# A transformer block in 32-token segments: three of four row tiles turned by DMA, the last MLP quarter finished tile by tile

## Chip, cores and metric

One core of one Trainium2 chip runs the kernel. The metric is device time in microseconds (us), a median over runs. A trace is one profiled execution. Engines: PE is TensorE (PEld its weight loads), DVE VectorE, ACT ScalarE, POOL GpSimd, SP SyncE, which only issues DMAs. A q behind the name (SPq, ACTq, POOLq) is the engine's queue of waits and DMA issues. "L497" is line 497 of the kernel before.

## What is computed

A recurrent attention over 64 segments of 32 tokens and an MLP read the same normalized rows, and both are added to the input. All is in bfloat16.

```python
x = A_x                                     # 1 x 2048 x 1024
xn = _layernorm(x, axis=-1)
return x + _A_ref(xn, ...) + _B_ref(xn, ...)

# _A_ref: 64 segments in order, 8 memory rows carried, 32 heads of 128
h = concatenate([mem, xs])                  # 40 x 1024
q, k, v = h @ Wq, h @ Wk, h @ Wv            # 1024 x 4096 each
p = softmax(mask(q @ k.T * scale))
o = (p @ v) @ Wo                            # 4096 x 1024
mem = o[:, :8]; outs.append(o[:, 8:])
# _B_ref
gelu(xn @ w1 + b1) @ w2 + b2                # 1024 x 3584 x 1024
```

## The kernel before

**The MLP comes first**, in four quarters of 512 rows, each of four row tiles of 128. `first_product` (L497) multiplies the 28 column blocks of w1 with the turned rows of the quarter, `xnT`, in eight matmuls each; ScalarE and VectorE make the GELU of each block. Then, in quarters 0 to 2, the second product (L618) runs tile by tile: 28 matmuls for each half of the columns, after which VectorE adds the bias (L625) and x (L626) into the x tile, and `keep_R` (L447) stores it to R_n in DRAM. In the same loop the next quarter's rows are made ready: `ln_apply` (L403) normalizes tile t, and after the tile's second half `turn_x` turns it by eight transposes on TensorE (L412) into PSUM and two copies to SBUF (L417), one on ScalarE and one on VectorE. At the quarter's end `keep_xT` stores the turned rows to DRAM (L430, L440) for the recurrence, with copies on GpSimd (L435) between, and `turn_R` (L484) issues some 14 small DMAs for each tile, which lay the sums of R_n out as the recurrence's residual rows; for the third quarter GpSimd issues them, for the fourth they go into a list `small` (L486).

The order of the work is that of the program text on each engine; DMAs leave in the order of their issuing queue. SP's queue holds at first the x rows, w1 and w2, then `keep_xT` of quarter 0, the x rows of quarter 1 (L344), 11 copies of streamed weights from DRAM to DRAM and five early weights (L246, L248), four `keep_R`, `keep_xT` and `turn_R` of the next quarter, then the next x rows, and so on.

**The last quarter** starts the recurrence's loads: each w1 block that is done with is overwritten by a weight unit of 512 KB. Its second product holds eight banks of PSUM (six named ps, two pT) for all four tiles at once. It begins with a bias matmul (ones x b2, L644) and a residual matmul (identity x x, L645) for each bank, then 28 steps of eight matmuls (L651); after each second step a w2 unit is done and `fetch_resident` loads a weight unit over it, after each fourth a gT unit. At the end eight copies (L665) on VectorE and ScalarE empty the banks, and four `keep_R` on ScalarE's queue store the rows. One of the ps banks holds the memory rows just before, until VectorE has copied them (L324).

**The recurrence** takes 64 segments. 47 of 64 weight units stay in SBUF, 17 are streamed in every segment through six places; a place is loaded again when its unit is done (`start_stream`, L278), on SP's queue. A segment makes K, Q and V in two halves (L769), scores, exponentials, and the O product (L1027); `put_mem` (L314) puts its new memory rows into the next segment's rows and marks the segment's end. Its own rows and residuals come by small loads: the next rows (L286), this segment's residuals (L1124) and, in each fourth segment, the residuals of the rows left over (L1150). VectorE adds the residuals to the output (L1184), and stores follow (L1190, L1218). The queue of these loads and stores is `loads`:

```python
loads = nc.scalar if s < EARLY_SEGS else nc.gpsimd      # EARLY_SEGS = 5
```

The list `small` is worked off by GpSimd, one or two DMAs after each streamed unit. After the last segment 12 stores, six on SP's queue and six on ScalarE's, write the output (L1207).

Of the kernel before, what the change touches and what calls it, by code (L numbers as in the profile page):

```python
# [17 lines left out]
P = 128  # L18
# [6 lines left out]
SEG = 32  # L25
# [23 lines left out]
SCRATCH = 320  # L49
SMALL = 3776  # L50
LEAD = 6
EARLY_SEGS = 5
LEAD_FIRST = 4
SCORES_0 = (6, 6, 6, 5)
SUMS_0 = (4, 4, 4, 4)
# [59 lines left out]
def kernel(  # L115
# [215 lines left out]
    with tc.tile_pool(name="ma", bufs=2) as ma, tc.tile_pool(name="mps", bufs=6, space=PSUM) as mps:  # L331
# [39 lines left out]
        for i in range(14):  # L371
            t = slab(f"w2_{i}")[:, :].rearrange("p (c d) -> p c d", d=DM)
            nc.sync.dma_start(out=t, in_=w2_v[:, 2 * i:2 * i + 2, :])
            w2_sb.append(t)

        mv = ma.tile([P, NT, 2], F32, name="ln_mv", bufs=1)
        rstd = ma.tile([P, NT], F32, name="ln_rstd", bufs=1)
# [44 lines left out]
        def turn_x(tt, xn, xnT):  # L422
            pT = turned(xn)
            for half in range(2):
                turned_out(tt, pT, half, xnT, nc.scalar.copy if (tt + half) % 2 else nc.vector.tensor_copy)

        def keep_xT(tg, xnT):
            xl = [t[:, 0:512].rearrange("p (g k i t) -> p g k i t", g=2, k=KT, i=GRP) for t in ko_flat]
            for half in range(2):
                nc.sync.dma_start(  # L430
                    out=rows_d[16 * tg:16 * tg + 16, :, 128 * half:128 * half + 128].rearrange("s p c -> p s c"),
                    in_=xnT[half].rearrange("p s k t -> p s (k t)"),
                )
                for g in range(4):
                    nc.gpsimd.tensor_copy(  # L435
                        out=xl[g // 2][:, g % 2, 4 * half:4 * half + 4, :, :],
                        in_=xnT[half][:, 4 * g:4 * g + 4, :, NX:SEG].rearrange("p i k t -> p k i t"),
                    )
            for k in range(2):
                nc.sync.dma_start(  # L440
                    out=rowsL_d[4 * tg + 2 * k:4 * tg + 2 * k + 2, :, :].rearrange("g p c -> p g c"),
                    in_=xl[k][:, :, :, :, :].rearrange("p g k i t -> p g (k i t)"),
                )

        def keep_R(ttg, rsb):
            eng = nc.scalar if ttg >= NT - 4 else nc.sync
            eng.dma_start(out=R_n[ttg * P:ttg * P + P, :], in_=rsb[:, :])  # L447

        def main_row(slot):
# [94 lines left out]
        for tg in range(4):  # L544
# [53 lines left out]
            if not last:  # L598
                xnT = new_xnT(tg + 1)
                for t in range(4):  # L600
                    xtoks[4 * tg + 4 + t] = load_x(4 * tg + 4 + t)
                if tg == 0:
                    for unit, c in copies.items():
                        fetch(c, unit)
                    fetch_resident(*EARLY)
                for t in range(4):
                    ln_stats(4 * tg + 4 + t)
                ln_sqrt(4 * tg + 4, 4 * tg + 8)
                ln_rstd(4 * tg + 4, 4 * tg + 8)
                for t in range(4):  # L610
                    ttg = 4 * tg + t
                    xn = ln_apply(ttg + 4)
                    rsb = xtoks[ttg]
                    for nb in range(2):
                        cs = slice(nb * 512, (nb + 1) * 512)
                        ps = mps.tile([P, 512], F32, name="ps")
                        for fc in range(FC):
                            nc.tensor.matmul(  # L618
                                ps[:, :],
                                lhsT=gts[fc // 4][:, fc % 4, t * P:(t + 1) * P],  # L620
                                rhs=w2_sb[fc // 2][:, fc % 2, cs],
                                start=(fc == 0),
                                stop=(fc == FC - 1),
                            )
                        nc.vector.tensor_tensor(out=ps[:, :], in0=ps[:, :], in1=b2bc[:, cs], op=ALU.add)  # L625
                        nc.vector.tensor_tensor(out=rsb[:, cs], in0=ps[:, :], in1=rsb[:, cs], op=ALU.add)  # L626
                        if nb == 1:
                            turn_x(ttg + 4, xn, xnT)
                    keep_R(ttg, rsb)
                keep_xT(tg + 1, xnT)  # L630
                for t in range(4):
                    turn_R(4 * tg + t, nc.gpsimd if tg == 2 else nc.sync)
            else:


                start_stream("xn2")
                start_stream("xn3")
                put_mem(o_sb, nxt["hT"], mps.tile([P, 512], F32, name="ps"), wide=False)
                nc.sync.dma_start(out=d_oL[:, 0:DM], in_=Wo_v[:, h + 1, :])
                pss = [mps.tile([P, 512], F32, name="ps") for _ in range(6)]  # L640
                pss += [mps.tile([P, 512], F32, name="pT", bufs=2) for _ in range(2)]
                for n in range(8):
                    cs = slice((n % 2) * 512, (n % 2 + 1) * 512)
                    nc.tensor.matmul(pss[n][:, :], lhsT=ones[0:1, :], rhs=b2row[0:1, cs], start=True, stop=False)  # L644
                    nc.tensor.matmul(  # L645
                        pss[n][:, :], lhsT=ident, rhs=xtoks[4 * tg + n // 2][:, cs], start=False, stop=False
                    )
                for fc in range(FC):
                    for t in range(4):
                        for nb in range(2):  # L650
                            nc.tensor.matmul(  # L651
                                pss[2 * t + nb][:, :],
                                lhsT=gts[fc // 4][:, fc % 4, t * P:(t + 1) * P],
                                rhs=w2_sb[fc // 2][:, fc % 2, nb * 512:nb * 512 + 512],
                                start=False,
                                stop=(fc == FC - 1),
                            )
                    if fc % 2:
                        fetch_resident(f"w2_{fc // 2}")
                    if fc % 4 == 3:  # L660
                        fetch_resident(f"gT{fc // 4}")
                for n in range(8):
                    cs = slice((n % 2) * 512, (n % 2 + 1) * 512)
                    cp = nc.scalar.copy if n % 2 else nc.vector.tensor_copy
                    cp(out=xtoks[4 * tg + n // 2][:, cs], in_=pss[n][:, :])  # L665
                for t in range(4):
                    keep_R(4 * tg + t, xtoks[4 * tg + t])

# [3 lines left out]
    with tc.tile_pool(name="late", bufs=1) as late, \  # L674
# [67 lines left out]
        for s in range(NSEG):  # L742
# [435 lines left out]
            for w, r in reversed(list(enumerate(tiles))):  # L1178
                if left_o:
                    o = psX[:, 256 * w:256 * w + 256].rearrange("p (h e) -> p h e", e=32)  # L1180
                else:
                    o = o_sb[:, 0:8, :]
                r_rows = r.rearrange("p (h e) -> p h e", e=32)
                nc.vector.tensor_tensor(out=r_rows, in0=o, in1=r_rows, op=ALU.add)  # L1184
                if left_o and not final:

                    for b in range(2):
                        c0 = 256 * (2 * b + w)
                        eng = nc.scalar if w else nc.gpsimd
                        eng.dma_start(out=outL_d[og, :, c0:c0 + 256], in_=r[64 * b:64 * b + 64, :])  # L1190
# [5 lines left out]
            if final:  # L1196
                engines = [nc.sync, nc.scalar]
                n = 0
                for w, r in enumerate(tiles):
                    for b in range(2):  # L1200
                        cs = slice(256 * (2 * b + w), 256 * (2 * b + w) + 256)
                        pieces = [(rows, slice(64 * b + m0, 64 * b + m0 + NX))]
                        for sl, row in left_rows:
                            p0 = 64 * b + NL * sl
                            pieces.append((slice(row, row + NL), slice(p0, p0 + NL)))
                        for o, i in pieces:
                            engines[n % 2].dma_start(out=out_flat[o, cs], in_=r[i, :])  # L1207
                            n += 1
            elif left_o:
                pairs = [(out_flat[rows, :], outL_d[og, m0:m0 + NX, :])]  # L1210
                pairs += [
                    (out_flat[row:row + NL, :], outL_d[og, NL * sl:NL * sl + NL, :]) for sl, row in left_rows
                ]
                for o, r in pairs:
                    small.append(lambda o=o, r=r: nc.gpsimd.dma_start(out=o, in_=r))
            else:
                for j in range(4):
                    loads.dma_start(out=out_flat[rows, 256 * j:256 * j + 256], in_=res[32 * j:32 * j + NX, :])  # L1218
# [37 lines left out]
```

## Time and profile before

| what | us |
|---|---|
| three runs | 1810.53, 1817.72, 1818.7 (median 1817.72) |
| the profiled execution | 1811.68, span 1809.9, mean granted clock 0.998 |
| MLP, span's start to the first matmul of the recurrence | 417.0 |
| TensorE busy | 1707.1 (94%) |
| VectorE, ScalarE, GpSimd busy | 978.1, 687.9, 305.2 |

The page's first part gives each engine's busy time, the second the span in 40 slices of 45 us: a digit is the busy share in tenths, PEclk the granted clock, DMA the share of the 16 DMA engines. The third part gives the DMA queues: 567.08 of 592.07 MB go through q1, SP's. The chain of work that ended last is followed back from the end; in order of time it reads as "start, length, what". A table by stretch gives the busy time of each engine between two times. In a timeline, brackets give the idle time ahead of an instruction and what ended it.

### The profile page before, as it was taken

The page shows a single profiled execution, that of the slowest core. Times are in us where ns is not written, and L with a number is a line of the kernel's source. Part 1 is how long each engine was busy: PE and PEld are TensorE (multiplying, and loading weights), DVE is VectorE, ACT ScalarE, POOL GpSimd, SP SyncE. Part 2 cuts the span into 40 slices and gives each one's busy share as a digit, 9 for nine tenths or more (in the row PEclk, how much of TensorE's full clock was granted, in tenths as well). Part 3 has the DMA queues.
Part 4 walks back from the last instruction along what each step waited for, and adds up shares of the span by engine and source line. Part 5 has one row for each costly group of instructions (what it writes and reads, how often), then busy time and mean ns, then how long its engine had stood idle before and what let it go on. Part 6 is the DMA issues. An engine that isn't in the chain of part 4 may idle for free.

```text
span 1809.9 us, 71522 instructions
## 1 busy us (share of the span) xinstructions
PE 1707.1 (94%) x31173; PEld 893.0 (49%) x31173; DVE 978.1 (54%) x2508; ACT 687.9 (38%) x1700; POOL 305.2 (17%) x595
## 2 busy tenths in 40 slices
PE   8999999998988999999999999999999999999997
PEld 4444444444444545545444555554545454555544
DVE  7657483804554555555555555555555555555554
ACT  6334260702333334333333334343433333434333
POOL 0000000411122211111111212111111111111111
PEclk9999999999999999999999999999999999999999
DMA  9931111769999999999999999999999999999997
GB/s 290 308 100 48 52 48 36 246 225 345 385 371 346 389 377 384 387 377 393 380 373 374 383 395 394 368 398 379 393 385 376 382 370 369 398 393 384 391 396 294
DMA packets 220870, 592.07 MB, mean 327 GB/s; under 512 B 46283, under 2 KB 75995, under 8 KB 220556
## 3 DMA queue, kind: packets, MB, share of 16 engines
q1 hardware_dynamic: 197652, 567.08, 83.5%
q0 software_dynamic: 17184, 17.23, 2.9%
q8 instruction: 244, 4.00, 0.9%
q10 hardware_dynamic: 5720, 3.19, 0.6%
q14 instruction: 70, 0.57, 0.1%
HBM read 573.43 MB, written 28.90 MB: 333 GB/s over the span
## 4 chain that ended last, share of the span: by engine, by line
PE 72%; DMA 13%; issue 6%; ACT 4%; DVE 3%; POOL 1%; ACTq 0%; DVEq 0%; POOLq 0%; SPq 0%
PE acc L769 34%; PE acc L1027 12%; PE ps L497 11%; PE ps L618 8%; DMA u<-Wc_O 7%; DMA u<-Wc_V 3%; PE ps L651 2%; ACT mixed L938 2%; PE acc L978 1%; DMA u<-Wc_Q 1%; PE mixed L886 1%; DVE kq L853 1%; DVE pd_main L951 1%; POOL res_d L486 1%; ACT kq L848 1%
## 5 line engine op out<-in xcount | busy, mean ns | idle before, releaser
L769 PE MATMUL acc<-u,hr_home 128*32 128x512 bf16 x11520 | 760.8, 380 | 15.7 <-issue 6.0
L769 PEld LDWEIGHTS <-hr_home 128*32 128x32 bf16 x12288 | 348.0, 96 | 285.5 <-issue 33.8
L769 PE MATMUL acc<-u,hrL 128*32 128x512 bf16 x2880 | 254.5, 380 | 4.4 <-issue 2.4
L497 PE MATMUL ps<-u 128*128 128x512 bf16 (+1 forms) x920 | 194.4, 373 | 2.0 <-ACT u L417 2.0
L267 DVE TENSOR_SCALAR u<-kept 128x512 uint32<-128x512 uint32 x254 | 163.1, 684 | 51.7 <-PE acc L769 39.2
L821 ACT CAST d_oL<-acc 128x512 bf16<-128x512 f32 x143 | 82.0, 585 | 261.0 <-PE acc L769 254.2
L618 PE MATMUL ps<-u 128*128 128x512 bf16 x672 | 147.0, 379 | 0.0
L1027 PEld LDWEIGHTS <-kq 128*32 128x32 bf16 x3908 | 103.1, 96 | 79.0 <-issue 22.2
L1027 PE MATMUL acc<-u,d_oL 128*32 128x512 bf16 x1944 | 133.9, 381 | 8.5 <-DMA u<-Wc_O 4.7
L497 PEld LDWEIGHTS <-u 128*128 128x128 bf16 x920 | 89.8, 98 | 104.9 <-issue 2.4
L1027 PE MATMUL acc<-u,kq 128*32 128x256 bf16 (+1 forms) x2372 | 117.2, 313 | 16.0 <-DMA u<-Wc_O 13.4
L853 DVE STREAM_TRANSPOSE kq<-kq 128x512 bf16<-128x512 bf16 x128 | 91.0, 711 | 74.8 <-ACT kq L848 72.6
L951 DVE TENSOR_TENSOR pd_main<-kq,mixed 128x320 bf16<-128x320 bf16 x128 | 62.4, 487 | 127.3 <-ACT mixed L938 127.3
L848 ACT CAST kq<-acc 128x512 bf16<-128x512 f32 (+2 forms) x192 | 85.3, 444 | 114.7 <-PE acc L769 85.1
L1218 POOL DMA_DIRECT2D out_dram<-hr_home x172 | 87.2, 514 | 227.3 <-DVE hr_home L1184 226.8
L825 ACT CAST kq<-acc 128x512 bf16<-128x512 f32 x128 | 75.2, 587 | 111.2 <-PE mixed L892 109.9
L769 PEld LDWEIGHTS <-hrL 128*32 128x32 bf16 x3072 | 86.3, 96 | 58.1 <-issue 5.9
L916 DVE TENSOR_TENSOR kq<-kq,mixed 128x96 bf16<-128x96 bf16 (+1 forms) x256 | 38.1, 190 | 125.7 <-ACT kq L906 70.5
L618 PEld LDWEIGHTS <-u 128*128 128x128 bf16 x672 | 65.3, 98 | 77.4 <-DVE g_u L579 0.4
L571 ACT ACTIVATE g_xb<-ps,b1col 128x512 bf16<-128x512 f32 x112 | 76.8, 686 | 55.6 <-PE ps L497 54.7
L938 ACT ACTIVATE mixed<-mixed,small_consts 128x160 f32<-128x160 f32 x256 | 94.2, 368 | 8.4
L1027 PEld LDWEIGHTS <-d_oL 128*32 128x32 bf16 x2592 | 63.8, 96 | 63.8 <-issue 16.1
(132 smaller groups left out, 2015.4 us busy)
## 6 DMA issues: line engine op xcount, KB each, us to landing
u<-Wc_K SPq DMA_DIRECT2D x256, 512.0 KB
u<-Wc_V SPq DMA_DIRECT2D x256, 512.0 KB
u<-Wc_O SPq DMA_DIRECT2D x256, 512.0 KB
u<-Wc_Q SPq DMA_DIRECT2D x192, 512.0 KB
u<-in_B_w_dram SPq DMA_DIRECT2D x28, 512.0 KB
u<-in_A_Wq_dram SPq DMA_DIRECT2D x13, 512.0 KB
u<-in_A_Wv_dram SPq DMA_DIRECT2D x12, 512.0 KB
u<-in_A_Wk_dram SPq DMA_DIRECT2D x9, 512.0 KB
```

The lines of the kernel that those rows point to most:

```text
L267: nc.vector.tensor_single_scalar(out=out, in_=in_, scalar=0, op=ALU.bitwise_or)
L497: nc.tensor.matmul(ps[:, SEG * s0:SEG * s1].rearrange("p (s t) -> p s t", t=SEG), lhsT=w1_sb[fb // 2][:, kt, (fb % 2) * P:(fb % 2 + 1) * P ...
L571: nc.scalar.activation(out=xb[:, :], in_=ps[:, :], func=ACT.Identity, bias=b1col[:, fb:fb + 1], scale=1.0)
L618: nc.tensor.matmul(ps[:, :], lhsT=gts[fc // 4][:, fc % 4, t * P:(t + 1) * P], rhs=w2_sb[fc // 2][:, fc % 2, cs], start=(fc == 0), stop=(fc ...
L769: nc.tensor.matmul(o, lhsT=lhs[:, i, :], rhs=m, start=(i == seq[0]), stop=(i == seq[-1]), tile_position=(0, 32 * j),)
L821: cp(out=out, in_=ps.rearrange("p (h e) -> p h e", e=32))
L848: nc.scalar.copy(out=q_home[:, h0:h1, NL:40], in_=ps[:, 32 * h0:32 * h1].rearrange("p (h e) -> p h e", e=32))
L853: nc.vector.transpose(out=home, in_=home)
L938: nc.scalar.activation(out=mixed[:, 160 * b:160 * b + 160], in_=mixed[:, 0:160], func=ACT.Exp, scale=-1.0, bias=off[:, b:b + 1],)
L951: nc.vector.tensor_tensor(out=pdA.rearrange("p c b q -> p b c q"), in0=prA[:, None, :, :].to_broadcast([P, 2, 4, 40]), in1=dd, op=ALU.mult,)
L1027: nc.tensor.matmul(acc[r0:r0 + rows, 0:256 * len(blocks)], lhsT=lhsT, skip_group_check=True, rhs=o_columns(t, k, blocks), start=start, sto ...
L1218: loads.dma_start(out=out_flat[rows, 256 * j:256 * j + 256], in_=res[32 * j:32 * j + NX, :])
```

## The change

- `send_x`: tiles 1 to 3 of the next quarter are turned by eight transposing DMAs each, on SP's queue, from 32 rows x 512 columns of the normalized tile straight into `xnT`. Tile 0 stays on TensorE. The DMAs of a tile are issued right after its `ln_apply`.
- The x rows are loaded a quarter ahead: those of quarter 1 before the first product of quarter 0, those of quarters 2 and 3 after the tile loops of quarters 0 and 1. The weight copies and early weights, which stood ahead of quarter 0's tile loop, stand behind it.
- `keep_R` of the first three tiles goes to ScalarE's queue in all quarters.
- Last quarter: 20 of the 28 steps run as before; then tile by tile. Tiles 0 to 2 get bias and x by VectorE's adds, and are stored at once; tile 3 keeps bias and residual matmuls, now in the middle. The weight loads of the last eight steps are issued in tile 3's second half. Tile 3's second half is copied in two parts by two engines.
- `EARLY_SEGS` 5 becomes 7: the small loads and stores of segments 5 and 6 go to ScalarE's queue.
- The last segment's sums are put side by side in one tile, and six stores of 512 columns write them.

```diff
-EARLY_SEGS = 5
+TAIL = 8
+EARLY_SEGS = 7
...
+        xtoks.update({tt: load_x(tt) for tt in range(4, 8)})
...
+        def send_x(t, xn, xnT):
+            for i in range(4):
+                for half in range(2):
+                    nc.sync.dma_start_transpose(
+                        out=xnT[half][:, 4 * t + i, :, :],
+                        in_=xn[SEG * i:SEG * i + SEG, 512 * half:512 * half + 512],
+                    )
...
-            eng = nc.scalar if ttg >= NT - 4 else nc.sync
+            eng = nc.scalar if ttg >= NT - 4 or ttg % 4 < 3 else nc.sync
...
             if not last:
                 xnT = new_xnT(tg + 1)
                 for t in range(4):
-                    xtoks[4 * tg + 4 + t] = load_x(4 * tg + 4 + t)
-                if tg == 0:
-                    for unit, c in copies.items():
-                        fetch(c, unit)
-                    fetch_resident(*EARLY)
...
                     xn = ln_apply(ttg + 4)
+                    if t > 0:
+                        send_x(t, xn, xnT)
...
-                        if nb == 1:
+                        if nb == 1 and t == 0:
                             turn_x(ttg + 4, xn, xnT)
                     keep_R(ttg, rsb)
+                xtoks.update({tt: load_x(tt) for tt in range(4 * tg + 8, min(4 * tg + 12, NT))})
+                if tg == 0:
+                    for unit, c in copies.items():
+                        fetch(c, unit)
+                    fetch_resident(*EARLY)
                 keep_xT(tg + 1, xnT)
...
+                for fc in range(FC - TAIL):
+                    for t in range(4):
+                        for nb in range(2):
+                            second_product(fc, t, nb, False)
+                    freed(fc)
+                for nb, cs in enumerate(halves_of):
+                    nc.tensor.matmul(pss[6 + nb][:, :], lhsT=ones[0:1, :], rhs=b2row[0:1, cs], start=False, stop=False)
+                for nb, cs in enumerate(halves_of):
+                    nc.tensor.matmul(pss[6 + nb][:, :], lhsT=ident, rhs=x[:, cs], start=False, stop=False)
+                for t in range(3):
+                    for fc in range(FC - TAIL, FC):
+                        for nb in range(2):
+                            second_product(fc, t, nb, fc == FC - 1)
+                    r = xtoks[4 * tg + t]
+                    for nb, cs in enumerate(halves_of):
+                        ps = pss[2 * t + nb]
+                        nc.vector.tensor_tensor(out=ps[:, :], in0=ps[:, :], in1=b2bc[:, cs], op=ALU.add)
+                        nc.vector.tensor_tensor(out=r[:, cs], in0=ps[:, :], in1=r[:, cs], op=ALU.add)
+                    keep_R(4 * tg + t, r)
+                for nb in range(2):
+                    for fc in range(FC - TAIL, FC):
+                        second_product(fc, 3, nb, fc == FC - 1)
+                        if nb:
+                            freed(fc)
+                    if nb == 0:
+                        nc.scalar.copy(out=x[:, 0:512], in_=pss[6][:, :])
+                nc.vector.tensor_copy(out=x[:, 512:768], in_=pss[7][:, 0:256])
+                nc.scalar.copy(out=x[:, 768:1024], in_=pss[7][:, 256:512])
+                keep_R(4 * tg + 3, x)
...
-                nc.vector.tensor_tensor(out=r_rows, in0=o, in1=r_rows, op=ALU.add)
+                to = d_oL[:, 256 * w:256 * w + 256].rearrange("p (h e) -> p h e", e=32) if final else r_rows
+                nc.vector.tensor_tensor(out=to, in0=o, in1=r_rows, op=ALU.add)
...
+                for b in range(2):
+                    cs = slice(512 * b, 512 * b + 512)
...
+                        engines[n % 2].dma_start(out=out_flat[o, cs], in_=d_oL[i, 0:512])
```

More of the change, by code (lines that the diff above doesn't have):

```diff
@@ L600 @@
                 for t in range(4):
-                    xtoks[4 * tg + 4 + t] = load_x(4 * tg + 4 + t)
-                if tg == 0:
-                    for unit, c in copies.items():
-                        fetch(c, unit)
-                    fetch_resident(*EARLY)
-                for t in range(4):
                     ln_stats(4 * tg + 4 + t)
@@ L641, with second_product, freed @@
                 pss += [mps.tile([P, 512], F32, name="pT", bufs=2) for _ in range(2)]
-                for n in range(8):
-                    cs = slice((n % 2) * 512, (n % 2 + 1) * 512)
-                    nc.tensor.matmul(pss[n][:, :], lhsT=ones[0:1, :], rhs=b2row[0:1, cs], start=True, stop=False)
+                halves_of = [slice(512 * nb, 512 * nb + 512) for nb in range(2)]
+                x = xtoks[4 * tg + 3]
+                def second_product(fc, t, nb, stop):
                     nc.tensor.matmul(
-                        pss[n][:, :], lhsT=ident, rhs=xtoks[4 * tg + n // 2][:, cs], start=False, stop=False
-                    )
[L648 to L657, printed above, removed]
+                        pss[2 * t + nb][:, :],
+                        lhsT=gts[fc // 4][:, fc % 4, t * P:(t + 1) * P],
+                        rhs=w2_sb[fc // 2][:, fc % 2, halves_of[nb]],
+                        start=(fc == 0),
+                        stop=stop,
+                    )
+                def freed(fc):
                     if fc % 2:
@@ L661 @@
                         fetch_resident(f"gT{fc // 4}")
[L662 to L667, printed above, removed]
+                for fc in range(FC - TAIL):
[27 more added lines that the diff above has]
+                keep_R(4 * tg + 3, x)
     with tc.tile_pool(name="late", bufs=1) as late, \
@@ L1198 @@
                 n = 0
[L1199 to L1208, printed above, removed]
+                for b in range(2):
+                    cs = slice(512 * b, 512 * b + 512)
+                    pieces = [(rows, slice(64 * b + m0, 64 * b + m0 + NX))]
+                    for sl, row in left_rows:
+                        p0 = 64 * b + NL * sl
+                        pieces.append((slice(row, row + NL), slice(p0, p0 + NL)))
+                    for o, i in pieces:
+                        engines[n % 2].dma_start(out=out_flat[o, cs], in_=d_oL[i, 0:512])
+                        n += 1
             elif left_o:
```

## The prediction

> **What bounds the kernel now.** I read the page's 40 slices first, then the chain of work that ended last, in order of time for the first 420 us, then the stretches in which it leaves TensorE.
>
> ```profile
> PE   8999999998988999999999999999999999999997
> DMA  9931111769999999999999999999999999999997
> PE 72%; DMA 13%; issue 6%; ACT 4%; DVE 3%; POOL 1%; ACTq 0%; DVEq 0%; POOLq 0%; SPq 0%
> ```
>
> TensorE is busy throughout. The DMA engines are idle in the MLP (slices 3 to 6) and full in the recurrence. So the MLP is bound by TensorE's instructions alone, and the recurrence by TensorE and transfers together. One MLP quarter's end, from the chain:
>
> ```profile
> 100.14 12.09 PE ps L618 x56
> 112.23 0.46 PE pT L412 x8
> 112.69 0.02 issue
> 112.71 0.59 ACT u L417
> 113.31 0.04 issue
> 113.35 48.51 PE ps L497 x224
> ```
>
> Four tiles of 12.1 us each end in eight transposes of 0.45 us on TensorE; the fourth then waits 0.67 us for ScalarE's copy, since the next quarter's first product reads it. Next the end of the last quarter and the first segment, in a table by stretch (length; busy time of PE, PEld, DVE, ACT, POOL with counts; granted clock; DMA share; GB/s):
>
> ```profile
> 366.20:368.40 2.20, 2.20 (x7) 0.81 (x6) 0.00 (x0) 0.00 (x0) 1.05 (x2) 0.50 0.70 273
> 368.40:415.60 47.20, 47.20 (x220) 21.34 (x218) 1.24 (x3) 1.03 (x3) 6.11 (x12) 1.00 0.68 219
> 415.60:419.00 3.40, 2.25 (x42) 1.18 (x44) 3.03 (x7) 1.85 (x4) 0.00 (x0) 1.00 0.43 128
> 419.00:446.00 27.00, 23.63 (x488) 12.18 (x481) 14.61 (x33) 7.58 (x21) 7.14 (x13) 1.00 1.04 396
> ```
>
> The transfers have slack until 419 and none after. Then the segments, by their last small matmul (L314). Segment 6 (562.6 to 588.3) is the odd one: 25.7 us, where segment 2, of the same kind, takes 21.2 (473.2 to 494.4) and segment 14 20.3 (737.9 to 758.2). The reason is GpSimd's queue at the end of segment 5 (timeline), and from 562 to 590 the waits behind it (us in total, times, longest):
>
> ```profile
> 554.67 0.55 POOL L486 DMA_DIRECT2D res_d<-R_n  x1 [2.88 <-issue]
> 555.24 0.55 POOL L486 DMA_DIRECT2D resL_d<-R_n  x1
> 556.57 0.59 POOL L286 DMA_DIRECT2D hr_home<-rows_d  x1 [0.78 <-DVE kq L956]
> 561.01 0.57 POOL L1124 DMA_DIRECT2D hr_home<-res_d  x1 [3.85 <-PE acc L1027]
> 562.25 0.55 POOL L1150 DMA_DIRECT2D pd_main<-resL_d  x1 [0.67 <-PE acc L1027]
> ```
>
> ```profile
> DVE pd_main L1184 <- DMA pd_main<-resL_d: 4.2, 1, 4.2
> PE acc L769 <- DVE hr_home L1184: 3.1, 1, 3.1
> ```
>
> GpSimd is still working off the residual copies of L486; its loads L1124 and L1150 leave at the segment's very end, VectorE waits for their landing, and TensorE behind it.
>
> **The change, part by part.** The sum is against the profiled execution, 1811.68 us (span 1809.9).
>
> *Tiles turned by DMA.* Nine groups of eight transposes leave TensorE: 9 x 0.45 = 4.05 us. Three waits of 0.67 us go, if the DMAs are in time: 2.0 us. Together 6.0, all on the path, since nothing else holds TensorE there. Their removed PSUM copies were idle-engine work and count nothing. The added cost is SP's and the DMA engines': eight transposing DMAs for each tile, 72 in all. Before shows none, so I bound the time k that one occupies SP and its queue. Below: 0.33, the shortest SP issue (the R_n store, L447). Above: 1.67, the median issue of rows_d (L430), a store of many small pieces. I take 0.61, SP's issue of the residual copies (L484), which are small and of short pieces like these; landing 1.8, the shortest of that row.
>
> When is that late? In quarters 0 and 2 the fourth tile's normalized rows are ready 1.9 us after the third tile's last matmul (from 74.63 to the end of L403 at 76.88, less 0.33 for L417's copy, which goes): of 12.1 us 10.2 remain, less the landing 8.4, so eight DMAs of k up to 1.05 are hidden, and all 24, from 76.9 to 111.3, too. In quarter 1 SP is behind. It now issues, after quarter 0, the copies and early weights (27.5 us from 58.91 in the trace), the stores of the turned rows (5.6) and 56 residual copies (119.77 to 155.5, 35.8). From about 114.7 that ends at 183.6, and some 3 us later for loads that have not landed, near 187. Quarter 1 ends at 111.3 (112.69 less three groups of transposes) + 48.5 + 4 x 12.1 + 0.45 = 208.6, so 24 DMAs have 21.6 us less the landing: k up to 0.82. At 0.61 both hold. In SP's order the R_n store and x loads follow the DMAs; nothing needs them before the next quarter's end. The copies, 40 us later than before, are first read in the last quarter.
>
> One rule speaks against this part: the Trainium skill, "VectorE: DVE Perf Modes", section "The three transpose paths", gives 390 ns for a 128x128 transpose on TensorE and 1309 ns by DMA. The trace's row for TensorE is 219 ns for one (L412, 0.45 for eight overlapped). By that 1.31 for k, quarter 1 would be late by 24 x 1.31 + 1.8 - 21.6 = 11.6 us and the others by 8 x 1.31 + 1.8 - 10.2 = 2.1 each, and this part would lose 9.8 us, not gain 6.0.
>
> *Last quarter.* Before, 16 bias and residual matmuls at 0.32 us run from 360.57, ten of them while bank six is held until 363.88 by the memory rows' copy on VectorE (L324). After, five product matmuls fit in before that bank stops TensorE, and four bias matmuls stay. From 363.92: 219 x 0.2157 + 4 x 0.32 = 48.5. The clock row above is 0.5 for about 3.3 us, which cost 1.65; TensorE idles more there now, so I keep it. End 414.1, was 415.7: 1.6 us gained, 3.3 if the clock holds, nothing if the wait costs a second window. The wait of 1.16 us before the first segment was four copies of 0.6 to 0.7 in a row on each of two engines; one copy of a half-width remains: 0.5 gained. The adds of the first three tiles (4 x 0.7 for each) lie under the next tile's 16 matmuls (3.5). Against it: three weight fetches and a half that were spread over 405 to 415 now leave together at the end, 1.8 MB into the full stretch, 4.6 us at 396 GB/s; three R_n stores (0.8 MB, 2.0 us) leave it, and the unused 1.9 us of 415.6 to 419 fills. Loss 0.7, bounds 0 and 3; I take 1.0. Net gain 1.1.
>
> *Segments 5 and 6 on ScalarE's queue.* Segment 2 is the row: same kind, loads on ScalarE, GpSimd's backlog running. 25.7 - 21.2 = 4.5, with 0.1 for the four stores no longer on GpSimd: 4.6. Bounds: nothing if ScalarE's issue is as late, 5.4 by segment 14. The price is ScalarE's four output stores ahead of its first copy, already in segment 2's time. GpSimd's backlog is over at 555, so segment 7 finds it free.
>
> *Six stores at the end.* Each queue issues three and not six; the last issue starts near 1805.2, was 1806.6: 1.4 us.
>
> Sum: 6.0 + 1.1 + 4.6 + 1.4 = 13.1, so 1798.6 for the profiled execution. That lies near the lowest of the three runs (1810.53); against the median, 1817.72, the same sum gives 1804.6. Of four executions two lie low and two high, so I predict the middle, **1802**.
>
> **Rivals.**
> - *Transposes somewhat late.* k = 1.14, midway between the rows: quarter 1 is late by 24 x 1.14 + 1.8 - 21.6 = 7.6, the others by 8 x 1.14 + 1.8 - 10.2 = 0.7: 9.0 of the 13.1 are gone, 1811 on the same middle. For it: SP's queue in quarter 1 has only 0.2 us to spare for each DMA. Against: the DMA engines are idle there (slices 3 to 6). The Trainium skill's 1309 ns would make it 1818, still no change that can be told.
> - *Slower: transposes hold the next quarter.* At k = 1.67, the rows_d row, late by 20.3 us in quarter 1 and by 24 x 1.67 + 1.8 - 34.4 = 7.5 in the others: 35.3 - 13.1 = 22 slower, 1837. It breaks even at k near 1.24 and passes 0.5% at 1.46. Place: the first weight load of L497 (L508 in the new file), which waits for the DMAs of the turned rows.
> - *The segment 6 stall stays*, because the load's place in the segment and not the queue is late: 8.5 gained, 1806.
>
> **How the numbers follow.** Forecast 0.54; somewhat late 0.20; stall stays 0.12; slower 0.14. A change under 0.5%, some 9 us, can't be told from none here, so the second and third are "same": faster 0.54, same 0.32, slower 0.14. Range: below, all parts at their best bound (6.0 + 3.8 + 5.4 + 1.9 = 17.1 off the lowest run), 1793; above, past the first rival, 1815.
>
> **What would show it.** Right: nine groups of L412 fewer on TensorE, L497's successor following the product with no gap; segment 6 near 21 us; three stores on each queue at the end. Wrong: TensorE waiting at a quarter's start for DMAs into the turned rows, above all at the second; SP's issue of a transposing DMA well over 0.8 us; waits for Wc_O in segment 0 growing beyond 1 us; a clock of 0.5 lasting longer than 3.3 us after 363.

## The result, and the profile after

The change makes the kernel slower. The medians of 14 runs each are 1824.6 us and, for the kernel before, 1812.3; the ratio, estimated from all these runs and not from the two medians, is 1.0056 with a 95% interval of 1.0039 to 1.0072, some 10 us. Forecast was 1802, 13 us gained. Line numbers from here on are those of the new file (L497 is now L508, L484 L495, L651 L658, L769 L802); L433 is the transposing DMA.

The profiled execution has a span of 1817.3. From the page of after: TensorE's busy tenths, its granted clock, the DMA share, and the chain's shares by engine.

```profile
PE   8999699998999999999999999999999999999998
PEclk9999899999999999999999999999999999999999
DMA  9455221778999999999999999999999999999998
PE 71%; DMA 13%; ACT 4%; DVE 4%; issue 4%; SPq 4%; ACTq 0%; DVEq 0%; POOL 0%; POOLq 0%
```

Slice 5 (182 to 227 us) has a 6 where before had a 9, and SP's queue, 0% of the chain before, holds 4% of it. Where the time went, from the first matmuls of each stage in the two timelines:

| stage | before | after | |
|---|---|---|---|
| start to quarter 3's first L508 | 312.0 | 322.5 | +10.5 |
| quarter 3, to the recurrence's first matmul | 105.0 | 101.6 | -3.4 |
| segment 0 | 34.3 | 38.8 | +4.5 |
| segments 1 to 6 | 137.0 | 131.7 | -5.3 |
| segments 7 to 62 | 1192.9 | 1196.8 | +3.9 |
| last segment and stores | 28.6 | 25.9 | -2.7 |

The first row is one wait, less what the change gains ahead of it. The longest wait of TensorE from 100 to 230 us (total, times, longest), and the chain around it:

```profile
PE ps L508 <- DMA u<-ln_xn: 13.7, 1, 13.7
```

```profile
219.96 1.24 SPq L433
221.19 0.04 issue
221.24 2.33 DMA u<-ln_xn
223.57 0.20 issue
223.76 49.89 PE ps L508 x224
```

Quarter 1's product ended at 210.1; quarter 2's began at 223.8, when the turned rows that its first matmuls read had landed. SP's queue tells why it was late (start, length, line, count):

```profile
77.48 35.00 SPq L433 DMA_TRANSPOSE u<-ln_xn  x24
...
144.62 8.97 SPq L441 DMA_DIRECT2D rows_d<-u  x2
...
156.47 1.34 SPq L495 DMA_DIRECT2D res_d<-R_n  x2
...
192.34 0.61 SPq L495 DMA_DIRECT2D resL_d<-R_n  x1
193.06 30.69 SPq L433 DMA_TRANSPOSE u<-ln_xn  x24
223.87 0.51 SPq L458 DMA_DIRECT2D R_n<-u  x1
```

In quarter 0 the 24 transposing DMAs are spread over 35 us, as their rows get ready. In quarter 1 the rows of tiles 1 and 2 are ready at 175.7 and 187.9 (VectorE's L405), but the queue is taken by the residual copies up to 193, and then 24 DMAs need 30.7 us back to back: 1.24 each, 1.28 from one to the next. And the wait has a second price, in the stretches behind it (length; busy time of PE, PEld, DVE, ACT, POOL with counts; granted clock; DMA share; GB/s):

```profile
210.00:223.00 13.00, 0.11 (x1) 0.00 (x0) 1.39 (x2) 0.00 (x0) 0.29 (x1) 0.61 0.12 25
223.00:226.00 3.00, 2.24 (x6) 0.87 (x7) 0.00 (x0) 0.00 (x0) 1.29 (x5) 0.50 0.42 109
226.00:228.00 2.00, 2.00 (x10) 0.78 (x8) 0.20 (x1) 0.69 (x1) 0.00 (x0) 0.85 0.95 280
228.00:240.00 12.00, 12.00 (x57) 5.44 (x56) 9.77 (x28) 9.47 (x15) 0.00 (x0) 1.00 0.66 168
```

TensorE begins again at half clock: quarter 2's first product takes 49.9 us where quarter 1's took 48.5 before, 1.4 more. The DMA engines are nearly idle through the wait (a share of 0.12), so it is not their load that holds the rows up.

### The profile page after: what moved, and what is told of

Its sections match the earlier page's. It is cut to its first block, busy times and chain, and to the rows that moved or that the text cites. A ratio compares the mean times of both kernels' runs of the same rounds, so it can differ in the third digit from the quotient of the medians.

```text
span 1817.3 us, 71443 instructions
## 1 busy us (share of the span) xinstructions
PE 1700.4 (94%) x31089; PEld 889.0 (49%) x31089; DVE 981.5 (54%) x2508; ACT 682.2 (38%) x1689; POOL 300.1 (17%) x586
## 4 chain that ended last, share of the span: by engine, by line
PE 71%; DMA 13%; ACT 4%; DVE 4%; issue 4%; SPq 4%; ACTq 0%; DVEq 0%; POOL 0%; POOLq 0%
PE acc L802 36%; PE acc L1060 12%; PE ps L508 10%; DMA u<-Wc_O 7%; PE ps L625 5%; DMA u<-Wc_V 3%; PE ps L658 2%; SPq L495 2%; ACT mixed L971 2%; SPq L433 1%; PE acc L1011 1%; PE mixed L919 1%; DVE kq L886 1%; DVE pd_main L984 1%; DMA u<-Wc_Q 1%
## 5 line engine op out<-in xcount | busy, mean ns | idle before, releaser
L802 PE MATMUL acc<-u,hr_home 128*32 128x512 bf16 x11520 | 759.2, 380 | 16.8 <-issue 6.7
L802 PEld LDWEIGHTS <-hr_home 128*32 128x32 bf16 x12288 | 347.7, 96 | 284.5 <-issue 36.2
L802 PE MATMUL acc<-u,hrL 128*32 128x512 bf16 x2880 | 253.0, 380 | 4.4 <-issue 2.0
L508 PE MATMUL ps<-u 128*128 128x512 bf16 (+1 forms) x920 | 197.8, 378 | 14.5 <-DMA u<-ln_xn 13.7
L508 PEld LDWEIGHTS <-u 128*128 128x128 bf16 x920 | 90.6, 99 | 120.7 <-issue 18.8
L802 PEld LDWEIGHTS <-hrL 128*32 128x32 bf16 x3072 | 87.5, 96 | 57.7 <-issue 3.8
```

Source lines behind the costliest of these rows:

```text
L508: nc.tensor.matmul(ps[:, SEG * s0:SEG * s1].rearrange("p (s t) -> p s t", t=SEG), lhsT=w1_sb[fb // 2][:, kt, (fb % 2) * P:(fb % 2 + 1) * P ...
L802: nc.tensor.matmul(o, lhsT=lhs[:, i, :], rhs=m, start=(i == seq[0]), stop=(i == seq[-1]), tile_position=(0, 32 * j),)
```

## Experiments

All are compared with the kernel before on the same chip; five rounds each, but three for x9. "Wait" is TensorE's at the start of quarter 2; us but for the ratios.

| run | ratio to before | 95% interval | wait | segment 0 | segment 6 | segments 7 to 62 |
|---|---|---|---|---|---|---|
| after | 1.0056 | 1.0039 to 1.0072 | 13.65 | 38.8 | 20.3 | 1196.8 |
| x1 | 1.0012 | 0.9991 to 1.0034 | 10.03 | 38.4 | 20.4 | 1204.8 |
| x2 | 0.9979 | 0.9959 to 0.9998 | 0.67 | 37.8 | 22.0 | 1201.0 |
| x3 | 1.0041 | 1.0017 to 1.0066 | 14.62 | 35.1 | 19.8 | 1200.3 |
| x4 | 1.0094 | 1.0062 to 1.0127 | 13.68 | 38.2 | 26.7 | 1201.0 |
| x5 | 0.9986 | 0.9965 to 1.0006 | 1.03 | 38.4 | 20.2 | 1201.5 |
| x6 | 0.9993 | 0.9967 to 1.0018 | 0.67 | 35.0 | 20.9 | 1202.3 |
| x7 | 0.9986 | 0.9960 to 1.0012 | 0.67 | 38.3 | 20.4 | 1207.7 |
| x8 | 1.0133 | 1.0096 to 1.0170 | 3.51 | 38.2 | 19.9 | 1201.3 |
| x9 | 0.9877 | 0.9840 to 0.9914 | 0.67 | 34.6 | 24.4 | 1183.4 |
| x10 | 1.0001 | 0.9975 to 1.0026 | 0.67 | 34.9 | 22.2 | 1193.9 |
| x11 | 0.9978 | 0.9953 to 1.0003 | 0.67 | 34.5 | 20.2 | 1201.1 |
| x12 | 0.9959 | 0.9940 to 0.9978 | 0.69 | 34.8 | 21.0 | 1204.4 |
| x13 | 0.9970 | 0.9948 to 0.9993 | 0.00 | 35.2 | 20.2 | 1205.5 |
| x14 | 0.9969 | 0.9945 to 0.9993 | 0.01 | 38.3 | 20.3 | 1191.5 |
| x15 | 0.9984 | 0.9961 to 1.0007 | 0.00 | 35.3 | 24.7 | 1210.7 |

**x1: another queue for the transposing DMAs.**

```diff
-                    nc.sync.dma_start_transpose(
+                    nc.scalar.dma_start_transpose(
```

> The changed kernel with its 72 transposing DMAs issued by ScalarE (nc.scalar) instead of SP; nothing else differs. Theory A (SP's queue): in quarter 1 the 24 transposing DMAs wait behind 56 residual copies until 193 us and then take 1.28 us each, so TensorE waits 13.65 us. ScalarE is nearly idle in the second product, so the wait in front of the second L508 falls under 1 us, the half clock after it (1.4 us) goes, and the time falls about 15 us below the changed kernel: near 1807, ratio to before 0.997. Rival B (the transposes' own pace): what takes the time is the transposing itself, wherever it is issued; then a wait of several us stays in quarter 1, and quarters 0 and 2 show waits too, since ScalarE also stores R_n: 1815 or more.

Neither: the wait is 10.0. The chain of x1 shows ScalarE's first transposing DMA of quarter 1:

```profile
178.76 0.62 SPq L495
179.38 0.04 issue
179.42 1.87 DMA resL_d<-R_n
181.30 0.02 issue
181.32 0.02 ACTq L433
181.33 0.04 issue
181.37 1.46 ACTq L433
```

ScalarE waits for a residual copy of SP's queue to land. In this program every DMA of SP and ScalarE counts on one of the same eight completion semaphores (100 to 107 in the trace), handed out in the order of the program's text, and waits for its predecessor on that semaphore: SP's copy of 179.42 and ScalarE's first transposing DMA both count on 101. So the 56 copies, which stand earlier in the text, hold up the other queue as well. And each transposing DMA takes 1.26 us in the median on ScalarE too (1.18 to 2.14).

**x2: all tiles turned on TensorE again,** the rest as changed.

```diff
-                    if t > 0:
-                        send_x(t, xn, xnT)
-                        if nb == 1 and t == 0:
+                        if nb == 1:
```

> The changed kernel with all four tiles turned on TensorE again; loads, last quarter, segments and stores as changed. Theory A: the first three quarters end where those of the kernel before do (quarter 3 begins near 312 instead of 322.5), so 10 us come back: 1812 to 1815 if the rest of the change is worth nothing, near 1807 if it keeps what the trace of after shows (last quarter -3.4, segments 1 to 6 -5.3, end -2.6, segment 0 +4.5). Rival C (the loss is elsewhere, in the burst of weights at the end of the last quarter): the time stays above 1818.

Theory A holds, C falls: quarter 3 begins at 313.0, and the 0.0077 between the two ratios is 14 us. The transposing DMAs are what makes this kernel slower.

**x5: quarter 0's 56 residual copies on GpSimd,** the transposes on SP as changed.

```diff
-                    turn_R(4 * tg + t, nc.gpsimd if tg == 2 else nc.sync)
+                    turn_R(4 * tg + t, nc.sync if tg == 1 else nc.gpsimd)
```

> The changed kernel with the 56 residual copies of quarter 0 issued by GpSimd, as those of quarter 2 are, and not by SP; the transposing DMAs stay on SP. Theory A2 (with ScalarE as issuer the first transposing DMA of quarter 1 still started only at 181.4, released by the landing of an SP residual copy, so the 56 residual copies ahead of it hold it back wherever it is issued): without them on the hardware queues the transposes start as their rows are ready, near 177, the wait of 13.65 us falls under 1, the half clock behind it goes, and the time falls 15 us below the changed kernel: near 1808, ratio to before 0.997. Rival B (pace: 24 transposes cannot pass in a quarter beside the residual copies, whoever issues them): a wait of 5 us or more stays, ratio 1.000 or more.

A2 holds. SP's queue in x5 has the same 24 DMAs, now from 175.6 and as spread as in quarter 0, and the wait is 1.0:

```profile
158.78 0.44 SPq L451 DMA_DIRECT2D rowsL_d<-kq  x1
175.55 35.42 SPq L433 DMA_TRANSPOSE u<-ln_xn  x24
211.43 0.35 SPq L458 DMA_DIRECT2D R_n<-u  x1
```

So the price of a DMA did not change; only its place in the queue did. The time falls by 0.0070, some 13 us (15 were expected).

**x7: transposing DMAs in quarters 0 and 2 only.** `send_x` where `t > 0 and tg != 1`, and `turn_x` else.

> The changed kernel with the rows of the second quarter boundary (quarter 1's second product) turned on TensorE, and those of the other two boundaries by DMA. Theory A: the wait of 13.65 us and its half clock go, 1.7 us of transposes and one copy wait come back: 13.3 us below the changed kernel, 1809 to 1811, and some 3 us below the kernel with all on TensorE: ratio to before 0.995 to 0.997. Rival B (quarters 0 and 2 lose something too that is not seen as a wait of TensorE): no better than all on TensorE, 0.998.

0.9986: as good as x5 and x2 within the intervals, so the place that theory A names is confirmed. Expected were 0.995 to 0.997: the 3 us by which it was to beat x2 cannot be seen in the runs, which fits rival B as well, though the trace has them (quarter 3 begins at 308.5 and not 313.0).

**x8: the transposing DMAs on two queues in turn.**

```diff
-                    nc.sync.dma_start_transpose(
+                    (nc.scalar if half else nc.sync).dma_start_transpose(
```

> The changed kernel with its transposing DMAs issued in turn by SP and ScalarE (one half of the columns each). Theory H (1.24 us is the price of each queue by itself): after SP is free at 193 the two queues turn the rows twice as fast, 24 in 15 to 16 us and not 30.8, so the wait in quarter 1 falls to 1 or less: ratio to before 0.997. Rival I (one unit does all the transposing, 1.24 us each, whoever issues): the 24 still take 30 us and the wait stays at 10 to 14: ratio 1.001 to 1.006.

Neither was tested, and it is worse. The program has a wait for all that the other queue has under way at each switch: four go on SP, then some 1.3 us pass, then four go on ScalarE, so each four take some 6.5 us. The second half of the columns comes last, so TensorE stops again four matmuls into a product (6.1 us in quarter 2, behind the 3.5 of the table). Its waits from 100 to 230:

```profile
PE ps L508 <- DMA u<-ln_xn: 15.8, 3, 6.2
```

A fourth, of 5.7, stands in quarter 3's product, which begins at 327.5 (322.5 in after).

The Trainium skill, "DMA: Bandwidth & Descriptors", section "Silent corruption: two transposing streams in flight at once", says that a second stream's first transpose must wait for the first one's full completion. The waits of x8 are of that kind; whether two queues could go side by side, no run here shows.

**x3: the last quarter's second product as before,** bias and residual by sixteen matmuls first, all tiles together, weights fetched step by step.

> The changed kernel with the last quarter's second product as before (sixteen bias and residual matmuls first, all four tiles together, weights fetched as each chunk is used up). Theory D (the fetches held back to the end cost segment 0 its 4.5 us): segment 0, from the first recurrence matmul to its last small matmul, falls from 38.8 to about 34.5, while the quarter itself grows from 101.6 to about 105: together 1 us less than the changed kernel, 1821 to 1824. Rival E (segment 0 is long for another reason, for instance the clock or the time at which GpSimd's copies run): segment 0 stays near 38.8 and the time grows by 3.4, near 1828.

D's place is right: segment 0 falls to 35.1. The quarter grows to 106.7, of which 3.4 is clock (0.50 from 376.1 to 382.9); the ratios differ by less than their intervals. Why segment 0 pays is in two stretches of 13 us, the last ones of the product, in after and then in x12 (below), which has the old last quarter:

```profile
409.00:422.00 13.00, 13.00 (x62) 5.90 (x61) 7.83 (x12) 0.00 (x0) 3.08 (x6) 1.00 0.38 131
```

```profile
397.00:410.00 13.00, 12.95 (x61) 5.88 (x60) 0.83 (x2) 0.61 (x2) 0.00 (x0) 1.00 0.69 230
```

In after, six weight fetches wait for the last tile and leave between 421.9 and 425.4. The 99 GB/s that are missing for 13 us are 1.3 MB, and the full stretch behind (1.04, 399 GB/s) needs 3.2 us for them. There TensorE waits, from 424 to 455:

```profile
PE acc L802 <- DMA u<-Wc_Q: 3.1, 2, 1.6
```

**x4: EARLY_SEGS 5 and twelve stores** in the changed kernel.

> The changed kernel with segments 5 and 6 loading on GpSimd again (EARLY_SEGS 5) and with twelve output stores at the end. Theory F: segment 6 grows from 20.3 to about 25.7 and the end by 1.4, so the time grows by 7: near 1831. Rival G: the backlog on GpSimd falls otherwise, since quarter 2 ends 10 us later, and segment 6 stays at 20 to 21: the time grows by 1.4 alone, near 1826.

F holds: the ratio is 0.0038 above that of after, 7 us as expected, segment 6 takes 26.7, and VectorE waits there as it did before, behind the late load on GpSimd:

```profile
DVE pd_main L1217 <- DMA pd_main<-resL_d: 4.2, 1, 4.2
```

The last segment and stores take 27.3, with six stores 25.9: 1.4.

**x6 and x11: EARLY_SEGS 7 and six stores alone,** in the kernel before, twice.

> The kernel before with two parts of the change alone: segments 5 and 6 loading on ScalarE (EARLY_SEGS 7) and six stores at the end. Theory F: segment 6 takes near 20.3 and not 25.7, and the end is 1.4 shorter: 6.8 us faster than before, ratio 0.996. Rival G (what segment 6 gains is taken back by the transfers, which are full in every segment): the segments 1 to 6 together take as long as before, 137 us, and only 1.4 stay: ratio 0.999.

> The kernel before with EARLY_SEGS 7 and six stores at the end, as already run once (0.9993), for a second measurement. Theory F with M: the part is worth 6.8 us, ratio 0.996, and the steady part comes out shorter than 1202.3. Rival G with N: the ratio stays at 0.999 and the steady part at 1200 or more: what segment 6 gains is given back later.

Segment 6 is short in both (20.9, 20.2), but the two ratios average 0.9986, 2.6 us and not 6.8, and their segments 7 to 62 took 1202.3 and 1201.1. That looked like rival G.

**x10: the kernel before, unchanged.**

> The kernel before, unchanged, for a second profile of it and to see what two equal kernels differ by. Theory M (the steady part, from segment 6's end to the last segment, varies by several us from one execution to the next, and the first profile's 1192.9 was a short one): its steady part comes out between 1195 and 1205, ratio 1.000. Rival N (the kernel before really has a shorter steady part than every kernel with a part of the change, which had 1197 to 1208): again 1191 to 1195.

1193.9, so N here; but segment 6 took 22.2 and not 25.7: the stall itself varies. VectorE's wait for the late load is 2.8 us in x10 and 4.2 in the first profile, and there a stretch of half clock follows it (569.8 to 573.3) that x10 does not have.

**x9: fewer bytes in the stream,** in the kernel before (half of each streamed V unit left out from segment 8 on).

```diff
-            nc.sync.dma_start(out=t[:, :], in_=copies[unit])
+            cols = 1024 if unit[0] == "V" and seg_of[n] >= 8 else 2048
+            nc.sync.dma_start(out=t[:, 0:cols], in_=copies[unit][:, 0:cols])
```

> The kernel before, but from segment 8 on each streamed weight unit of the V projection is copied by half (its first 1024 columns), and the product reads that half twice: the same matmuls and the same DMAs in number, some 13% fewer bytes in the stream. It leaves out half of the V weights, so the output differs. Theory K (from segment 0 on the transfers set the pace, so that what TensorE gains there or ahead of it is mostly not seen at the end): the segments get shorter by what TensorE idles in them, some 4 to 5%, 45 to 60 us in all. Rival L (TensorE and its chain of dependences set the pace): under 15 us.

Between the two: 0.9877, 22 us, 1.6% of the recurrence's 1393 us. From 600 to 1700 us the DMA share falls from 1.00 to 0.95, and TensorE's busy time rises only from 1039.1 to 1045.0 us of 1100. So these bytes are part of the pace; what sets the rest is not shown.

**x12, x13, x14, x15: the copies of quarter 0 on GpSimd,** with the old last quarter (x12, x13), the new one (x14, and x5 above), and the old one with EARLY_SEGS 5 (x15).

> The changed kernel with quarter 0's residual copies on GpSimd (which took the wait of quarter 1 away) and the last quarter as before. Theory D (what the new last quarter gains, segment 0 pays): within 2 us of the same kernel with the new last quarter, ratio 0.997 to 1.000, with segment 0 near 35 and the last quarter near 105. Rival: the new last quarter is worth its 3.4 us: ratio 1.000 to 1.002; or it costs, and the ratio is 0.996 or less.

> Quarter 0's residual copies on GpSimd and the last quarter as before, a second measurement (first: 0.9959), beside the same with the new last quarter. Theory D2 (the new last quarter costs: what it gains goes to segment 0, and more): again 0.995 to 0.997, and below the next run by 0.002 or more. Rival D (the two cancel): the two runs agree within 0.001.

> Quarter 0's residual copies on GpSimd with the new last quarter, a second measurement (first: 0.9986). Theory D2: 0.998 to 1.000 again. Rival D: 0.996 to 0.997, as the run beside it.

> As the first of these three, but segments 5 and 6 load on GpSimd again (EARLY_SEGS 5). Theory F (these loads are worth what the first profile's segment 6 showed, 4.6): ratio 0.0025 above the first. Theory F2 (that profile caught a long stall; a second profile of the kernel before had 22.2 in segment 6 and not 25.7): segment 6 between 22 and 26, ratio 0.001 to 0.0015 above the first.

Old against new last quarter: 0.9959 and 0.9970 against 0.9986 and 0.9969; side by side (x13, x14) they are equal, as D has it. Over the three pairs there are (with x3 and after) the old one is ahead by 0.0014 on average, less than the intervals, so that a cost of 2 or 3 us is not excluded. x15 is 0.0014 above x13, as F2 expected, but the intervals are wider than that. x14 settles what the ledger lacked: it is x5 over again, and its segments 7 to 62 took 1191.5, where x5's took 1201.5. From 600 to 1700 us in x14, then in x15:

```profile
600.00:1700.00 1100.00, 1042.50 (x23563) 566.28 (x23559) 595.29 (x1537) 426.43 (x1165) 204.58 (x388) 1.00 1.01 385
```

```profile
600.00:1700.00 1100.00, 1032.39 (x23136) 556.89 (x23129) 585.38 (x1512) 417.67 (x1140) 201.41 (x382) 1.00 1.00 378
```

These segments run the same instructions in both; at a DMA share of 1 one execution moves 385 GB/s and the other 378, and the steady part differs by 19 us (1191.5, 1210.7). So the +3.9 in the ledger is within what executions differ by. N falls, since x14 has the change and is shorter still, and G is not needed. The clock explains little: in x15 it is at 0.50 for one stretch of 3.4 us between 600 and 1700, in x5 and x14 never. What sets the rate of an execution stays open.

x12 and x13, one program run twice, are the best of this study that compute the whole result: 0.9959 and 0.9970, both intervals below 1, 5 to 7 us faster than before. x14 is as good (0.9969), but x5, the same program, was 0.9986.

## Why the prediction was wrong

- **The price of a transposing DMA: the step that failed.** "I take 0.61, SP's issue of the residual copies" is 1.24 to 1.28, nearly the same on either queue. The row was chosen because the transfers look alike (small, short pieces); between bounds of 0.33 and 1.67 no row spoke for a transpose. With 1.28 the prediction's own sum for quarter 1 gives 24 x 1.28 + 1.8 - 21.6 = 10.9 us late. The other 2.8: SP was free at 193.1 and not 187 (the stores of the turned rows took 11.8 and not 5.6), +6.1; the first matmuls read only the first half of the columns and so wait for the last DMA but one, -1.8; the product ended at 210.1 and not 208.6, -1.5. Together 13.7, measured 13.65.
- The Trainium skill's rule against this part ("VectorE: DVE Perf Modes", section "The three transpose paths", 1309 ns for a 128x128) was right: each DMA here turns as many elements, 32 x 512, in 1.24 to 1.28. By it the part was to lose 9.8; quarter 3 began 10.5 late. That the sums agree so well is luck: the 2.1 that the rule adds in each of quarters 0 and 2 did not come (waits of 0.6 and 0.0), and quarter 1 lost more, since SP was late. The prediction had the sum and gave it too small a chance.
- **The rival "transposes hold the next quarter"** is what happened, in its place (the second quarter boundary, L508, DMAs into the turned rows); its break-even of 1.24 was too high, since it counted on gains of 13.1 and on SP being free at 187: at 1.24 to 1.28 the kernel lost 10. Quarters 0 and 2 hide their DMAs, as forecast, but barely: with 1.28 the prediction's sum would have them late by 1.8, and what saves them is that the first matmuls wait only for the last DMA but one.
- Not counted: the half clock after the wait, 1.4.
- **The gain of the nine groups.** Where the wait is gone, quarter 3 begins at 306.8 to 308.6 (x5, x12, x13, x14) against 312.0 and 312.2 before: 4.2 of the 6.0.
- **Last quarter:** forecast 2.1 gained and 1.0 lost. It gained 3.4 in the first pair of profiles, half of it luck with the clock: after held 1.00 there (the prediction's best case), before had its stretch of 3.4 us at 0.50. At like clock the gain is 1.7: with no such stretch the old quarter takes 103.3 (x9, x11) and the new one 101.6; with one, 105.0 and 103.3 (x4, x7). Segment 0 lost 3.1 to 4.5, above the upper bound of 3: not three and a half fetches but six were held back. The net is near zero or a small loss, and the runs (x12 and x13 against x5 and x14) cannot tell which.
- **Segments 5 and 6:** forecast 4.6. Segment 6 takes 22.2 to 26.7 with GpSimd's loads (five profiles, mean 24.7) and 19.8 to 22.0 with ScalarE's (twelve, mean 20.5): 4.2. Right in place, and in size by the traces. The runs show between 2.5 (x13 against x15) and, with the stores, 2.6 (x6 and x11) and 7 us (x4 against after), with intervals as wide. A part is clock, which the prediction did not see: a stretch of 3.4 us at 0.50 lies in segment 6 in four of the five profiles (before, x4, x9, x15), but in only one of the twelve (x2, which has the 22.0).
- **Six stores:** forecast 1.4, measured 1.4 (x4 against after) to 2.7 (the ledger).

Without the first point, x5 and x14 are what the forecast was about: 0.9986 and 0.9969, 4 us and not 13. The terms as the traces show them leave 4.2 + 0 + 4.2 + 1.4 = 9.8; the runs' intervals reach 4 us to either side, and the steady part's spread is of that size. Whether the other 6 are noise or lost somewhere stays open.

Of the signs named ahead, the wait at the second quarter and the SP issue over 0.8 us came; the waits that grew in segment 0 were for Wc_Q, not Wc_O, and the half clock came at another place.

## What to carry to other kernels

A move from a busy engine to an idle queue is priced by that queue's time for each DMA and by what stands in it ahead: count both at every place where the result is due, the worst first. When an operation has no row in the trace and its bounds straddle the break-even, the break-even is the forecast's real number, and a measured figure for that very operation outweighs the row that looks alike. Loads held back ahead of a stretch that is full of transfers are paid for there. And before a stage's gain between two profiles is put down to the change, compare the granted clock in that stage.

## What the runs showed of the hardware

- A transposing DMA of 32 KB keeps its issuing queue for 1.24 us in the median on SP and 1.26 on ScalarE (x1): 26 GB/s, while the DMA engines' share is 0.17 (77 to 112 and 193 to 224 us of after). Plain residual copies of 8 to 64 KB take 0.61 in the median.
- After 13.65 us without matmuls TensorE ran at a granted clock of 0.50 for some 3 us.
- The granted clock falls to 0.50 for stretches of 3.4 us, at other places in each execution: from 365.0 and from 569.8 us in before, from 458.7 in after, from 444.3 in x5, nowhere up to 1794 us in x14.
- Two executions of one program (x5 and x14), both at a granted clock of 1.00 from 600 to 1700 us, differ by 10 us in the same 56 segments, with a DMA share of 1.00 and 1.01 there.
